# A cached-attention decode kernel on one core: V moves from SyncE's DMA queue to ScalarE's

## The chip, the core and the metric

The kernel runs on one core of a Trainium2 chip. That core has five engines with their own instruction streams: TensorE (PE, matrix products), VectorE (DVE), ScalarE (ACT), GpSimd (POOL) and SyncE (SP). Sixteen DMA engines carry data between HBM and the on-chip memory SBUF; an engine starts a transfer by an instruction in its own stream, and the transfers that one engine issues form a queue. A transfer raises a semaphore when it has landed, and any engine can wait for that. The metric is the time on the device in microseconds, as the median over runs.

## The reference: what is computed

One token for each of 4 batch entries goes through an attention block and a gated feed-forward block:

```
h  = x + softmax(q K^T / sqrt(128)) V @ wo      with q = layernorm(x) @ wq
h2 = h + (sigmoid(n @ w_gate) * (n @ w_up)) @ w_down      with n = layernorm(h)
x: [4, 1, 512]     K and V caches: [4, 32 heads, 8192, 128], bf16
```

K and V together are 537 MB of the 551 MB that the kernel reads. Every byte of them is used once.

## The kernel before, in words

The 128 pairs of batch entry and head are cut into 32 *units* of four heads (`NU`). For a unit, K is one transfer of 128 partitions by 64 KB (8.39 MB) and V is another. SBUF holds three such *slots*: K of unit u goes to slot u % 2, V to slot 2, and V of the last unit to slot 0. Slot 2 first holds the weights `wq`, slot 1 at the end `wo`, `w_gate` and `w_up`, and slot 2 at the end `w_down`.

In `unit(u)` the work of one unit is emitted in this order:

- `scores(u)`: VectorE transposes K in 16 pieces (L334), and TensorE multiplies each piece with q (L343).
- `maxima(u)`: first a tiny memset on VectorE (L360), which stands behind the last transpose and whose token `t_kd[u]` says that the K slot is free. Then the row maximum, and the exponential on ScalarE (L368).
- `pv(u - 1)`: the product of the previous unit's weights with its V, 64 matmuls on TensorE (L404), whose token is `t_pv`; ScalarE copies the result, scaled, to SBUF (L409), and TensorE collects it (L414) in two steps. The token of the first step is `t_vd[u - 1]`, that of the second is `t_ex[u - 1]`.
- `weights(u)`: VectorE transposes the exponentials into `PTz` (L374). It waits for `t_ex[u - 1]`, since the matmuls of `pv(u - 1)` read `PTz`. The transposes of the next unit's K stand behind it in VectorE's stream.

So `pv(u - 1)` needs two things: V of unit u-1 has landed, and the scores of unit u are done. The next K transposes need K landed and, by the order of VectorE's stream, `pv(u - 1)` done.

All the large transfers are issued by SyncE in one order written out by hand (L224 and L531 to L557): `wq`, K0, K1, V0, K2, V1, K3, V2 and so on to K31, V30, V31, then the later weights. SyncE works through the list in order and waits before each issue: K of unit u for `t_kd[u - 2]`, V of unit u for `t_vd[u - 1]`, V0 for `t_qp`, which says that `wq` has been used. The last V waits for `t_kd[30]`, `wo`, `w_gate` and `w_up` for `t_kd[31]`, and `w_down` for `t_vd[30]`. Because the list has one order, a K whose slot is free waits until the V ahead of it has been issued.

From unit 1 on, the streams of TensorE, VectorE and ScalarE are hardware loops: VectorE and ScalarE have 15 turns of two units each (units 1 to 30), TensorE 31 turns of one unit.

Of the kernel before, what the change touches and what calls it, by code (L numbers as in the profile page):

```python
# [18 lines left out]
class _Prog:  # L19
# [52 lines left out]
    def emit(self, eng, fn, waits=(), incs=1, ch=None):  # L72
        todo = self._waits(eng, waits)
        key = ch or eng
        tok = self.token(key, incs) if incs else None
        self._put(eng, todo, key, fn, incs, 1)
        return tok
# [41 lines left out]
def bass_sequential_preLN__mha_block_cached__glu_gated_glu__decode_kernel(  # L119
# [12 lines left out]
    B, _sq, D = A_x.shape  # L132
# [6 lines left out]
    HU = 4  # L139
    NU = B * H // HU  # L140
    R = S // 32
    SLOT = R * DH
# [11 lines left out]
    prog = _Prog({"p2d": "dve", "d2d": "dve", "a2d": "dve", "d2p": "pe", "a2p": "pe",  # L154
                  "d2a": "act", "p2a": "act",
                  "k0": "dve", "k1": "dve", "v2": "pe"})
    emit = prog.emit

    with ExitStack() as es:
# [3 lines left out]
        def raw(t):  # L163
            return t.tensor if hasattr(t, "tensor") else t
# [34 lines left out]
        def reg(slot, off, size):  # L199
            return KV[:, slot * SLOT + off:slot * SLOT + off + size]  # L200
# [20 lines left out]
        for k in keys:  # L221
            prog.sems[k] = es.enter_context(nc.semaphore("s_" + k))

        order = [("k", 0)] + [x for u in range(1, NU) for x in (("k", u), ("v", u - 1))] + [("v", NU - 1)]  # L224
        slots = {(x, u): (0 if u == NU - 1 else 2) if x == "v" else u % 2 for x, u in order}
        toks = {x: prog.token(x[0] + str(slots[x]), 16) for x in order}
        t_wq = prog.token("wq", 16)
        t_wo = prog.token("wo", 16)
        t_wg = prog.token("wg", 16)
# [64 lines left out]
        for g in range(2):  # L294
# [8 lines left out]
            t_qp = emit("pe", f, [t_wq, t_xn, t_ps0, t_selc], incs=4)  # L303

            src = bank[QB[g]].rearrange("p (k w r) -> p r k w", k=8, r=2)
# [6 lines left out]
        t_tr, t_sc, t_pv, t_ex, t_mx, t_exp, t_ptz, t_lq, t_ocp, t_rs, t_kd, t_vd, t_sum = ({} for _ in range(13))  # L312
# [4 lines left out]
        def at(ix, d):  # L317
            return ix[d] if len(ix) > d else 0
# [5 lines left out]
        def q_window(u, t=0):  # L324
            dst = bass.AP(raw(Lq), 15, [[528, 128], [128, 4], [16, 8]])
            msk = bass.AP(raw(mask), 0, [[8, 128], [0, 4], [1, 8]])
            t_lq[u] = emit("dve", lambda e, ix: e.tensor_tensor(  # L327
                dst, bass.AP(raw(q_all), at(ix, 0) * (4 * TU) + 4 * (u - TU * t), [[NU * 4, 128], [1, 4], [0, 8]]), msk, ALU.mult),
                           [t_q, t_lq0, t_mask, t_sc.get((u - 1, NT - 1))], ch="d2p")
# [51 lines left out]
        def filler(n, turns=1):  # L381
# [9 lines left out]
            if turns > 1:  # L391
                prog.close("pe")

        def pv(u, t):
            t_rs[u] = emit("dve", lambda e: e.reciprocal(rsb[:, :], bank[QB[1]][:, 1:2]), [t_sum[u]], ch="d2a")  # L395
            slot = slots["v", u]
            ob = 512 * OBK

            def f(e, ks):
                made = []  # L400
                for k in ks:
                    j, n, r4 = k % 4, k // 4, k % 4
                    lhsT = PTz[:, 512 * r4 + n:512 * r4 + n + 481:32]
                    made.append(e.matmul(PS[32 * j:32 * j + 16, ob:ob + 512], lhsT,  # L404
                                         KV[:, slot * SLOT + 512 * k:slot * SLOT + 512 * (k + 1)],
                                         start=(k < 4), stop=(k >= 60), tile_position=(0, 32 * j)))
                return made[-4:]
            t_pv[u] = emit("pe", lambda e: f(e, range(64)), [toks["v", u], t_ps0], incs=4, ch="p2a")
            t_ocp[u] = emit("act", lambda e: e.activation(O_sb, bank[OBK], ACT.Copy, scale=rsb[:, 0:1]), [t_pv[u], t_rs[u]], ch="a2p")  # L409

            def fs(e, ix, qs):
                ins = None
                for q in qs:
                    ins = e.matmul(bass.AP(raw(PS), at(ix, 0) * 4 + (512 * EX + 4 * (u - t)), [[4096, 128], [1, 4]]),  # L414
                                   O_sb[:, 128 * q:128 * (q + 1)], lane[:, q:q + 13:4],
                                   start=False, stop=(u == NU - 1 and q == 3), skip_group_check=True)
                return ins
            t_vd[u] = emit("pe", lambda e, ix: fs(e, ix, (0,)), [t_ocp[u], t_selc, t_ps0], ch="p2x")
            t_ex[u] = emit("pe", lambda e, ix: fs(e, ix, (1, 2, 3)), ch="p2d")

        def unit(u, t=0):
            scores(u)
            maxima(u)
            if u + 1 < NU:
                q_window(u + 1, t)
            else:
                emit("dve", lambda e: e.memset(dummy[:, 3:4], 0.0), ch="d2p")
            if u:
                pv(u - 1, u - 1)
            weights(u)  # L430

        emit("pe", lambda e: e.matmul(bank[EX][:, 0:128], PTz[:, 0:128], PTz[:, 0:128], start=True, stop=False,
                                      skip_group_check=True), [t_pool, t_ps0], incs=0)
        q_window(0)
        unit(0)

        prog.open("pe", "dve", "act")
        for u in range(1, NU):
            t, first = divmod(u - 1, TU)
            if u == NU - 1:  # L440
                prog.close("dve", "act")
                t = 0
            elif not first:
                prog.begin("dve", "act")
            prog.begin("pe")
            unit(u, t)
            prog.end("pe")
            if first:
                prog.end("dve", "act")
        prog.close("pe")  # L450
        filler(2, 12)
        pv(NU - 1, 0)
        t_oa = emit("dve", lambda e: e.tensor_tensor(  # L453
            OA.rearrange("p (n k) -> p n k", k=4), bass.AP(raw(PS), 512 * EX, [[4096, 128], [1, 128], [0, 4]]),
# [69 lines left out]
        for t in range(NFT):  # L524
            if t == 0:
# [4 lines left out]

        prog.dma("sp", "wq", lambda e: e.dma_start(reg(2, 0, NC * H * DH), A_wq.rearrange("(p c) f -> p (c f)", p=128)),  # L531
                 tok=t_wq)
        for n, (x, u) in enumerate(order):
            w = t_qp if n == 2 else None
            if n >= 3:
                w = t_kd[u - 2] if x == "k" else t_kd[NU - 2] if u == NU - 1 else t_vd[u - 1]
            slot = slots[x, u]
            cache = A_v_cache if x == "v" else A_k_cache
            src = cache[u // (NU // B), HU * (u % (NU // B)):HU * (u % (NU // B) + 1), :, :].rearrange("h (p r) d -> (h p) (r d)", p=32)
            prog.dma("sp", f"{x}{slot}", lambda e, src=src, slot=slot: e.dma_start(reg(slot, 0, SLOT), src), [w],  # L540
                     tok=toks[x, u])
        for _ in range(40):
            emit("sp", lambda e: e.nop(), ch="pad")
        k_done, v_done = t_kd[NU - 1], t_vd[NU - 2]
# [46 lines left out]
```

## Time and profile before

| what | value |
|---|---|
| time, median of 3 runs | 1279.48 us (1279.21 to 1279.5) |
| span of the profiled execution | 1277.7 us |
| PE busy | 797.8 us (62%) |
| DVE busy | 763.3 us (60%) |
| ACT busy | 58.9 us (5%) |
| bytes read | 550.77 MB, 431 GB/s over the span |
| share of the span in which the 16 DMA engines moved packets of SyncE's queue | 99.7% |

The span runs from the first to the last instruction that the profiler saw; the time of a run holds 1.8 us more. "Busy" counts instructions in execution. In the chain of waits each step is followed back to what released it, so a long DMA step there means that an engine waited for that transfer. A transfer's time "to landing" runs from its issue and so includes the time behind other transfers of its queue. In rows of the timeline, the brackets give the idle time ahead of an instruction and what ended it; SPq and ACTq are the streams in which SyncE and ScalarE issue transfers.

### The profile page before, as it was taken

What the parts mean: (1) busy time and instruction counts of PE and PEld (TensorE: products, weight loads), DVE (VectorE), ACT (ScalarE), POOL (GpSimd) and SP (SyncE); (2) the same over time, 40 slices, a digit from 0 to 9 for tenths busy, and PEclk for the clock granted to TensorE, in tenths of its full rate; (3) what the DMA queues carried; (4) which work ended last, traced back from release to release, by engine and by line L of the source; (5) the groups of instructions that cost most, each with busy time, mean ns of one, the idle gap of its engine ahead of it and who ended that gap; (6) DMA issues with size and microseconds to landing.
All of it is one profiled execution on the core that took longest, in us unless ns stands there. A gap on an engine that the chain in (4) does not pass through costs nothing. (4 is left out here: it accounts for less than half of the span.)

```text
span 1277.7 us, 14121 instructions
## 1 busy us (share of the span) xinstructions
PE 797.8 (62%) x4636; PEld 327.1 (26%) x4636; DVE 763.3 (60%) x917; ACT 58.9 (5%) x114; POOL 5.7 (0%) x22
## 2 busy tenths in 40 slices
PE   1676765557755557655567655567555576555578
PEld 0232222222222223222222222222222232222233
DVE  1876665556665557665567655566655566655571
ACT  2000000000000000000000000000000000000001
POOL 1000000000000000000000000000000000000000
PEclk9988877788877788877788777788777888777888
DMA  9999999999999999999999999999999999999998
GB/s 427 427 425 429 427 455 427 431 427 435 447 427 431 427 437 445 427 431 427 445 437 429 429 427 451 431 429 429 427 453 429 429 429 427 455 427 429 429 429 368
DMA packets 10244, 550.83 MB, mean 431 GB/s; under 512 B 1144, under 2 KB 1152, under 8 KB 1408
## 3 DMA queue, kind: packets, MB, share of 16 engines
q1 hardware_dynamic: 10224, 550.77, 99.7%
q8 instruction: 2, 0.03, 0.0%
q14 instruction: 2, 0.02, 0.0%
q10 hardware_dynamic: 16, 0.01, 0.0%
HBM read 550.77 MB, written 0.00 MB: 431 GB/s over the span
## 5 line engine op out<-in xcount | busy, mean ns | idle before, releaser
L334 DVE STREAM_TRANSPOSE kT<-KV 128x1024 f32<-128x1024 f32 x512 | 615.1, 1233 | 301.1 <-DMA KV<-in_A_k_cache_dram 241.0
L343 PE MATMUL PS<-kT,Lq 128*128 128x512 bf16 x2048 | 586.1, 417 | 320.2 <-DVE kT L334 302.6
L343 PEld LDWEIGHTS PS<-kT,Lq 128*128 x2048 | 209.6, 102 | 697.0 <-issue 623.6
L374 DVE STREAM_TRANSPOSE PTz<-E_sb 32x512 bf16<-32x512 bf16 x128 | 89.9, 703 | 128.9 <-PE PS L414 125.2
L404 PE MATMUL PS<-KV,PTz 128*16 128x512 bf16 x2048 | 116.9, 381 | 0.0
L378 PE MATMUL PS<-part,headw 128*128 128x2 f32 x64 | 18.7, 362 | 100.5 <-DVE PTz L374 100.5
L368 ACT ACTIVATE E_sb<-PS,negm 128x512 bf16<-128x512 f32 x32 | 22.0, 687 | 1141.2 <-DVE negm L366 1141.2
L404 PEld LDWEIGHTS PS<-KV,PTz 128*16 128x16 bf16 x2048 | 58.3, 109 | 56.8 <-issue 13.2
L414 PE MATMUL PS<-lane,kT 128*128 128x4 f32 x256 | 33.6, 255 | 30.9 <-ACT kT L409 30.9
L361 DVE TENSOR_REDUCE part<-PS 128x1 f32<-128x512 f32 x32 | 22.1, 692 | 38.8 <-PE PS L343 38.8
L414 PEld LDWEIGHTS PS<-lane,kT 128*128 128x128 f32 x256 | 31.0, 191 | 46.3 <-issue 44.9
L378 PEld LDWEIGHTS PS<-part,headw 128*128 128x128 f32 x64 | 16.0, 310 | 103.7 <-DVE PTz L374 103.7
L321 PE MATMUL PS<-Lq,headw 128*128 128x512 bf16 x32 | 18.7, 585 | 10.9 <-issue 9.5
L409 ACT ACTIVATE kT<-PS,rsb 128x512 f32<-128x512 f32 x32 | 22.0, 687 | 61.1 <-PE PS L404 61.1
L387 PE MATMUL PS<-Lq 128*128 128x512 bf16 x44 | 13.7, 478 | 0.2 <-issue 0.2
L327 DVE TENSOR_TENSOR Lq<-q_all,mask 128x32 bf16<-128x32 bf16 x32 | 9.7, 303 | 0.0
L453 DVE TENSOR_TENSOR kT<-PS,mask 128x512 bf16<-128x512 f32 x1 | 0.7, 692 | 12.9 <-PE PS L414 12.9
L366 DVE STREAM_TRANSPOSE negm<-mxr 128x32 f32<-128x32 f32 x32 | 6.8, 212 | 1.1
L363 DVE STREAM_TRANSPOSE turn<-part 128x32 f32<-128x32 f32 x32 | 6.8, 212 | 1.1
L387 PEld LDWEIGHTS PS<-Lq 128*128 128x128 bf16 x44 | 4.8, 115 | 8.2 <-issue 5.8
L395 DVE RECIPROCAL rsb<-PS 128x1 f32<-128x1 f32 x32 | 6.5, 202 | 0.7 <-PE PS L378 0.7
L300 PE MATMUL PS<-KV,kT 128*4 128x512 bf16 x32 | 3.6, 627 | 5.1 <-DMA KV<-in_A_wq_dram 5.1
(70 smaller groups left out, 59.5 us busy)
## 6 DMA issues: line engine op xcount, KB each, us to landing
KV<-in_A_wq_dram SPq DMA_DIRECT2D x1, 4096.0 KB, 12.2
KV<-in_A_wo_dram SPq DMA_DIRECT2D x1, 4096.0 KB, 27.5
KV<-in_B_w_gate_dram SPq DMA_DIRECT2D x1, 1792.0 KB, 31.4
KV<-in_B_w_up_dram SPq DMA_DIRECT2D x1, 1792.0 KB, 35.2
KV<-in_B_w_down_dram SPq DMA_DIRECT2D x1, 1024.0 KB, 32.5
KV<-in_A_k_cache_dram SPq DMA_DIRECT2D x32, 49.8
KV<-in_A_v_cache_dram SPq DMA_DIRECT2D x32, 30.8
KV<-in_B_w_down_dram SPq DMA_DIRECT2D x1, 512.0 KB, 33.3
```

What stands on the lines that cost most here:

```text
L321: emit("pe", lambda e: e.matmul(bank[bk], headb, zeros, start=True, stop=False, skip_group_check=True), waits, incs=0)
L327: t_lq[u] = emit("dve", lambda e, ix: e.tensor_tensor(dst, bass.AP(raw(q_all), at(ix, 0) * (4 * TU) + 4 * (u - TU * t), [[NU * 4, 128], [1 ...
L334: t_tr[u, c] = emit("dve", lambda e: e.transpose(kT[:, (c % 2) * TW:(c % 2 + 1) * TW], KVw[:, o:o + TW]), w, ch="d2p")
L343: ins = e.matmul(bank[SBK], bass.AP(raw(Lq), ix[-1] * 2 + (128 * t + c % 2), [[528, 128], [1, 128]]), rhs, start=False, stop=False, skip_g ...
L361: a = emit("dve", lambda e: e.tensor_reduce(part[:, 0:1], bank[SBK], AX.X, ALU.max), [t_sc[u, NT - 1], t_pool], ch="d2d")
L368: t_exp[u] = emit("act", lambda e: e.activation(E_sb[:, :], bank[SBK], ACT.Exp, bias=negm[:, 0:1], scale=SCALE, accum_out=part[:, 1:2]), [ ...
L374: return [e.transpose(PTz[32 * q:32 * (q + 1), :].rearrange("p (r q c) -> p r q c", r=4, q=4)[:, :, q, :], E_sb[32 * q:32 * (q + 1), :].re ...
L378: t_sum[u] = emit("pe", lambda e: e.matmul(bank[QB[1]][:, 0:2], headw[:, :], part[:, 0:2], start=True, stop=True), [t_ptz[u], t_selc], ch= ...
L387: emit("pe", lambda e: [e.matmul(bank[XS], Lq[:, 0:128], Lq[:, 0:512], start=True, stop=True) for _ in range(n)][-1], [t_ps0, t_lq[NU - 1] ...
L404: made.append(e.matmul(PS[32 * j:32 * j + 16, ob:ob + 512], lhsT, KV[:, slot * SLOT + 512 * k:slot * SLOT + 512 * (k + 1)], start=(k < 4), ...
L409: t_ocp[u] = emit("act", lambda e: e.activation(O_sb, bank[OBK], ACT.Copy, scale=rsb[:, 0:1]), [t_pv[u], t_rs[u]], ch="a2p")
L414: ins = e.matmul(bass.AP(raw(PS), at(ix, 0) * 4 + (512 * EX + 4 * (u - t)), [[4096, 128], [1, 4]]), O_sb[:, 128 * q:128 * (q + 1)], lane[: ...
```

## The change

A helper `load` issues one K or V transfer, or a range of columns of it, from a chosen engine. ScalarE issues V0 (with the wait for `t_qp`) ahead of unit 0, and V of unit u+1 inside `pv(u)`, between the 64 matmuls and ScalarE's own copy of their result, with the wait for `t_pv[u]` in place of `t_vd[u]`; this goes up to V28. SyncE issues `wq`, all of K without a V in between, then V29, the first half of V31, V30 and the second half of V31, and then the later weights as before. ScalarE's stream is no longer in the loop of 15 turns: it is unrolled. The slots are as before.

```diff
-        order = [("k", 0)] + [x for u in range(1, NU) for x in (("k", u), ("v", u - 1))] + [("v", NU - 1)]
+        order = [(x, u) for u in range(NU) for x in "kv"]
         slots = {(x, u): (0 if u == NU - 1 else 2) if x == "v" else u % 2 for x, u in order}
-        toks = {x: prog.token(x[0] + str(slots[x]), 16) for x in order}
+        toks = {x: prog.token(x[0] + str(slots[x]), 16 + 16 * (x == ("v", NU - 1))) for x in order}
+        APART = NU - 3
...
+        def load(eng, x, u, w, a=0, b=SLOT):
+            slot = slots[x, u]
+            cache = A_v_cache if x == "v" else A_k_cache
+            src = cache[u // (NU // B), HU * (u % (NU // B)):HU * (u % (NU // B) + 1), :, :].rearrange("h (p r) d -> (h p) (r d)", p=32)
+            prog.dma(eng, f"{x}{slot}", lambda e: e.dma_start(reg(slot, a, b - a), src[:, a:b]), [w], tok=toks[x, u])
...
             t_pv[u] = emit("pe", lambda e: f(e, range(64)), [toks["v", u], t_ps0], incs=4, ch="p2a")
+            if u + 1 < APART:
+                load("act", "v", u + 1, t_pv[u])
             t_ocp[u] = emit("act", lambda e: e.activation(O_sb, bank[OBK], ACT.Copy, scale=rsb[:, 0:1]), [t_pv[u], t_rs[u]], ch="a2p")
...
+        load("act", "v", 0, t_qp)
         q_window(0)
         unit(0)
 
-        prog.open("pe", "dve", "act")
+        prog.open("pe", "dve")
...
-        for n, (x, u) in enumerate(order):
-            w = t_qp if n == 2 else None
-            if n >= 3:
-                w = t_kd[u - 2] if x == "k" else t_kd[NU - 2] if u == NU - 1 else t_vd[u - 1]
...
+        for u in range(NU):
+            load("sp", "k", u, t_kd[u - 2] if u > 1 else None)
+        load("sp", "v", NU - 3, t_vd[NU - 4])
+        load("sp", "v", NU - 1, t_kd[NU - 2], 0, SLOT // 2)
+        load("sp", "v", NU - 2, t_vd[NU - 3])
+        load("sp", "v", NU - 1, t_kd[NU - 2], SLOT // 2)
```

More of the change, by code (lines that the diff above doesn't have):

```diff
@@ L440, in bass_sequential_preLN__mha_block_cached__glu_gated_glu__decode_kernel @@
             if u == NU - 1:
-                prog.close("dve", "act")
+                prog.close("dve")
                 t = 0
             elif not first:
-                prog.begin("dve", "act")
+                prog.begin("dve")
             prog.begin("pe")
@@ L448, in bass_sequential_preLN__mha_block_cached__glu_gated_glu__decode_kernel @@
             if first:
-                prog.end("dve", "act")
+                prog.end("dve")
         prog.close("pe")
@@ L532, in bass_sequential_preLN__mha_block_cached__glu_gated_glu__decode_kernel @@
                  tok=t_wq)
-        for n, (x, u) in enumerate(order):
-            w = t_qp if n == 2 else None
-            if n >= 3:
-                w = t_kd[u - 2] if x == "k" else t_kd[NU - 2] if u == NU - 1 else t_vd[u - 1]
[L537 to L541, printed above, removed]
+        for u in range(NU):
[4 more added lines that the diff above has]
+        load("sp", "v", NU - 1, t_kd[NU - 2], SLOT // 2)
         for _ in range(40):
```

## The prediction

> **What bounds the kernel now.** I read the page first, then busy time by stages, SyncE's waits, and the chain of waits.
>
> ```profile
> span 1277.7 us, 14121 instructions
> ...
> DMA  9999999999999999999999999999999999999998
> ...
> q1 hardware_dynamic: 10224, 550.77, 99.7%
> ```
>
> The 16 DMA engines move packets of one queue for 99.7% of the span. In three stretches of whole units (the last two columns are DMA share and GB/s):
>
> ```profile
> 100.00:138.70 38.70, 23.88 (x137) 9.92 (x138) 23.02 (x29) 1.47 (x3) 0.00 (x0) 0.78 1.00 434
> 500.00:887.00 387.00, 240.95 (x1392) 99.56 (x1392) 235.25 (x282) 14.65 (x30) 0.00 (x0) 0.81 1.00 434
> 1000.00:1193.50 193.50, 120.79 (x694) 49.76 (x694) 117.74 (x141) 7.32 (x15) 0.00 (x0) 0.81 1.00 434
> ```
>
> Always 1.00 and 434 GB/s, while PE, DVE and ACT have room. SyncE's longest wait looks like a fault that the change would mend, K held back behind V:
>
> ```profile
> SPq L540 <- PE PS L414: 1124.4, 30, 38.5
> ```
>
> The chain of waits shows that it costs nothing:
>
> ```profile
> 1008.94 0.33 SPq L540
> 1009.27 0.04 issue
> 1009.31 49.78 DMA KV<-in_A_k_cache_dram
> ...
> 1241.51 33.33 DMA KV<-in_B_w_down_dram
> 1274.84 0.04 issue
> ```
>
> One unit of the timeline (transposes of K26, `pv(25)`, the issues of V26 and K28, the landing of K27), then the landing of K31:
>
> ```profile
> 1020.41 2.37 DVE L334 STREAM_TRANSPOSE kT<-KV 128x1024 f32<-128x1024 f32 x2 [7.82 <-DMA KV<-in_A_k_cache_dram]
> 1041.04 0.06 DVE L360 MEMSET dumm<- 128x1 f32 x1
> 1042.20 3.65 PE L404 MATMUL PS<-KV,PTz 128*16 128x512 bf16 x64
> 1045.98 0.69 ACT L409 ACTIVATE kT<-PS,rsb 128x512 f32<-128x512 f32 x1 [1.45 <-PE PS L404]
> 1047.24 0.33 SPq L540 DMA_DIRECT2D KV<-in_A_v_cache_dram  x1
> 1047.61 0.43 SPq L540 DMA_DIRECT2D KV<-in_A_k_cache_dram  x1
> 1047.98 2.90 DVE L374 STREAM_TRANSPOSE PTz<-E_sb 32x512 bf16<-32x512 bf16 x4 [4.04 <-PE PS L414]
> 1059.12 2.37 DVE L334 STREAM_TRANSPOSE kT<-KV 128x1024 f32<-128x1024 f32 x2 [8.23 <-DMA KV<-in_A_k_cache_dram]
> ...
> 1213.92 2.37 DVE L334 STREAM_TRANSPOSE kT<-KV 128x1024 f32<-128x1024 f32 x2 [7.60 <-DMA KV<-in_A_k_cache_dram]
> ```
>
> From the landing of K26 (1020.41) to that of K31 (1213.92) are five units: 38.70 us each, so F = 19.35 us for one load of 8.39 MB, 433.5 GB/s. K27, issued at 1009.31 behind V25, takes 49.78 us to land: 11.1 for the rest of K26, then 2 F = 38.7. Nothing is left over, so the queue never runs dry; when a K is issued, 11 us of work still lie ahead of it. All 550.77 MB at that rate take 1270.5 us, and from the first issue of `wq` (0.80, quoted below) to the last landing (1274.84) are 1274.0. Only 3.5 us could be saved by keeping the engines fed, and they lie at the start. The order of issues has nothing more to give; it can only open gaps, or change the rate.
>
> **The change part by part.** I ask of each edit whether the engines run dry. I assume that two queues with work share an engine evenly (all K and V packets are alike) and that the sum stays 433.5 GB/s. From K's issue without V in its way, SyncE issues K28 at `t_kd` (1041.1) instead of 1047.61: 6.5 us earlier into a queue that had 11 us of work. Worth 0.
>
> *The start.* Rows that carry it:
>
> ```profile
> 0.80 0.56 ACTq L234 DMA_DIRECT2D KV<-in_A_x_dram  x1
> 0.80 0.38 SPq L531 DMA_DIRECT2D KV<-in_A_wq_dram  x1
> 2.86 0.68 DVE L272 BATCH_NORM_STATS2 kT<-KV 4x6 f32<-4x512 bf16 x1 [2.86 <-DMA KV<-in_A_x_dram]
> 13.01 3.58 PE L300 MATMUL PS<-KV,kT 128*4 128x512 bf16 x32 [5.06 <-DMA KV<-in_A_wq_dram]
> 16.71 0.33 SPq L540 DMA_DIRECT2D KV<-in_A_v_cache_dram  x1
> 32.32 2.37 DVE L334 STREAM_TRANSPOSE kT<-KV 128x1024 f32<-128x1024 f32 x2 [14.25 <-DMA KV<-in_A_k_cache_dram]
> 53.34 0.06 DVE L360 MEMSET dumm<- 128x1 f32 x1
> 53.43 0.33 SPq L540 DMA_DIRECT2D KV<-in_A_k_cache_dram  x1
> 59.80 2.37 DVE L334 STREAM_TRANSPOSE kT<-KV 128x1024 f32<-128x1024 f32 x2
> 80.82 0.06 DVE L360 MEMSET dumm<- 128x1 f32 x1
> 91.53 1.25 DVE L334 STREAM_TRANSPOSE kT<-KV 128x1024 f32<-128x1024 f32 x1 [0.86 <-DMA KV<-in_A_k_cache_dram]
> ```
>
> The price a of a queue that starts empty: `x` (4 KB) takes 2.06 us from issue to use; `wq` (4.19 MB, 9.68 us at the rate) takes 12.21, so 2.5. I take 2.1 to 2.5.
>
> Before, V0 is issued at 16.71 but lies behind K0 and K1. Now it has its own queue and shares with K0 from 16.7 + 2.1 = 18.8. K0 started F before its landing, at 12.95; 5.85 of its 19.35 us are done, the other 13.5 take 27.0. K0 lands at 45.8 instead of 32.3. Unit 0's weights end 27.5 us after K0 lands (59.80 - 32.32): 73.3. K1 lands when the bytes of K0, V0 and K1 are through, at 12.95 + 3 F = 71.0, before that. The transposes of K1 run from 73.3 and free their slot 21.0 later (80.82 - 59.80): 94.3, where it was 80.8. K3 needs that slot; its first data come at 94.4 + a = 96.5 to 96.9. What lies ahead is the same work as before (`wq`, K0, K1, V0, K2), so K2 lands at 91.5 as before. V1 can't fill the gap: it waits for `pv(0)`, which needs the scores of unit 1 and ends at 94.3 + 1.2 + 3.65 = 99.1. **The engines stand idle from 91.5 to 96.5 or 96.9: 5.0 to 5.4 us, taken as 5.2.** The work that covered V1's late issue, V0 still in the queue, is gone.
>
> *The steady units.* Let p be the end of `pv(u-1)`. ScalarE issues V(u) there, 1.4 us earlier than SyncE did (1047.24, where L404 ends at 1045.85). Behind the issue on ScalarE stands the copy L409, and behind that L414, L374 and the next transposes, so all come 0.56 us later (the issue of `x` on ScalarE); no DMA engine waits for that if a queue has work. `PTz` is done at p + 5.0 + 0.56 (1050.88 - 1045.85), the next slot is free 20.7 us later (1041.04 - 1020.41): p + 26.3. A gap opens if V(u) and the rest r of K(u+2) are through before that, so when r < 26.3 - F = 6.95. After the start K has been alone from `t_kd` until V's first data: 1.16 (1042.20 - 1041.04) + 3.65, so r = 14.5. K and V then share; V still has F - r left when K(u+3) joins, shares again, and K runs alone for 3.65 + a, so the next r is 14.5 - 5.95 = 8.6. From there the same working gives r' = 26.3 - 3.65 - 2.3 - r = 11.8, then 8.6, 11.8 and so on. Always above 6.95: **no gap, 0 us**, units alternating long and short with the mean at 38.7. The margin is 1.6 us, thin.
>
> *ScalarE unrolled.* Apart from the new issues it executes the same instructions with the same waits; 0 us here. K2 lands 59.2 us after K0 where 3 F are 58.05, so something once cost 1.15 us; I keep that as the upper bound for fetching a longer stream.
>
> *The end.* V29 goes behind K31 with the old wait. When it lands at L, V30 may be issued at L + 5.05 (1047.24 - 1042.20), and the first half of V31 fills the queue to L + 9.7. That covers it by 4.6 us. The second half of V31 then runs to L + 38.7; `wo`, which waits for `t_kd[31]`, is issued near L + 29.5. No gap. After the last V come the same weights, and the end follows the last landing as now. 0 us.
>
> **Sum** against the profiled execution: 1277.7 + 5.2 = 1282.9; the median of the runs is 1.8 above its span, so 1284.7.
>
> *A rule on the rate.* The Trainium skill (DMA: Bandwidth & Descriptors, "Where 436 GB/s comes from") gives 435.2 GB/s as the ceiling of the 16 ports; the trace's 433.5 lies 0.4% under it. By that page an estimate for a perfect second queue is 1265.5 us in place of 1270.5, so 5.0 back and a sum of 1279.7.
>
> **The rivals.**
>
> *Whole loads take turns.* An engine might finish one queue's load before it turns to the other. Then V0 goes between K0 and K1: K0 lands at 32.3, K1 at 71.0, its slot is free at 92.0, K3's data come at 94.2 to 94.6, and the gap is 2.9: 1282.4. For it: nothing in the views, which show no engine with two full queues. The Trainium skill has the rule (DMA: Bandwidth & Descriptors, "Queues, rings and completion order"): an engine drains a packet of several descriptors from one ring before it switches. No run here shows how large such a packet is. 12%.
>
> *The early V0 costs nothing*: K0 and K1, long in the queue, go first. K1's slot is free at 80.8, K3 in time, and the result is 1279.5. 7%.
>
> *The rate rises a little.* From K31's landing to that of `w_down`, V30, V31 and the weights (26.48 MB) take 60.92 us, 434.7 GB/s. Over the 1180 us in which two queues run (18.8 to about 1200), 0.28% is 3.3 us: 1281.4. 14%.
>
> *The rate rises enough: faster.* Two queues could leave no pause between two packets of an engine. It decides from 5.2 + 2.6 = 7.8 us on, so 0.66% or 436.4 GB/s; at 437.5 the time is 1273.9. Against: three stretches of one to ten units all show 434, as a hard limit would. For: the DMA share of 1.00 says that packets lie end to end, not that each could not be quicker. 10%.
>
> *V gets less than half, or two queues disturb each other.* At 45 to 55, V has only 11.9 us done when K(u+2) ends; the rest shares with K(u+3), K alone takes 5.95 again, the next r is 4.3, and 2.65 us of gap open in every second unit; at the start K0 lands earlier and the gap there is 2.9: 15 x 2.65 + 2.9 = 43, 1322. V with more than half only lengthens the start. And if sharing cost 2% (1.15 in 58.05, the one lag seen), 24 us come on top: 1308. Half such a disturbance gives 1296. For: the margin of 1.6 us. Against: the packets of K and V are alike. 17%.
>
> **How the numbers follow.** The forecast (even sharing, the same rate) has 40%, with 1282.5 to 1287 as its own range. Two tenths of a per cent, 2.6 us, is about what these runs can tell from no change: faster is below 1276.9, slower above 1282.0. Faster: the 10% of the higher rate and 2 for no gap with a slightly higher rate. Same: 14 - 1 for the small rise, 7 - 1 for the free start, 5 of the whole loads. Slower: the rest, 64. The range leaves out most of the faster case below and the heavier half of the disturbances above: 1276.5 to 1296.
>
> **What would show it.** Right: K0 lands near 46, the first transposes of K1 start near 73, and the DMA row or a window over 90 to 98 us shows a hole of some 5 us; from 100 us on the stretches of two units show 434 GB/s and 1.00, alternating short and long; the last landing stands 2.9 us ahead of the end. Wrong: 434 replaced by another figure in those stretches (a rate that depends on the number of queues), holes that recur every second unit (uneven shares), or K0 landing still at 32 (no early sharing).

## The result and the profile after

The changed kernel takes 1321.74 us in the median (1320.39 to 1324.57), the kernel before 1279.35: a ratio of 1.0336, with a 95% interval of 1.0324 to 1.0348. It is 42.4 us slower. The forecast was 1284.7, the range ended at 1296: the direction was right and the size far too small.

The page of the changed kernel, in the same parts as shown of before:

```profile
span 1320.6 us, 13984 instructions
...
DMA  9989999999999999999999999999999999998995
...
q1 hardware_dynamic: 6192, 307.50, 54.6%
q10 hardware_dynamic: 4192, 243.28, 42.6%
```

Two queues now carry the bytes: q1 is SyncE's, with K, the last V loads and the weights, and q10 is ScalarE's, with V0 to V28. Together they are busy for 97.2% of the span in place of 99.7%. VectorE's wait for the collected product with V (the transposes of the weights behind L423) has grown to three times. In the waits of the changed kernel, with total, times and longest:

```profile
DVE PTz L375 <- PE PS L423: 387.9, 31, 22.3
```

and of the kernel before:

```profile
DVE PTz L374 <- PE PS L414: 125.2, 31, 4.2
```

Busy time by stages of the changed kernel (the last two columns are DMA share and GB/s) shows four places where time went:

```profile
88.00:98.00 10.00, 8.52 (x84) 3.52 (x82) 5.91 (x12) 0.98 (x3) 0.00 (x0) 1.00 0.57 216
98.00:1200.00 1102.00, 675.57 (x3778) 278.10 (x3807) 652.02 (x772) 40.06 (x82) 0.00 (x0) 0.81 0.99 423
1200.00:1212.00 12.00, 10.17 (x94) 4.54 (x92) 7.03 (x13) 1.47 (x3) 0.00 (x0) 1.00 0.68 273
1308.00:1320.60 12.60, 9.05 (x108) 3.52 (x100) 3.88 (x10) 3.77 (x7) 0.00 (x0) 0.99 0.01 5
```

The same long stretch of the kernel before, and its last 12.6 us:

```profile
98.00:1200.00 1102.00, 691.34 (x3988) 284.60 (x3990) 675.59 (x804) 41.79 (x86) 0.00 (x0) 0.81 1.00 433
...
1265.10:1277.70 12.60, 8.27 (x88) 2.89 (x80) 3.87 (x10) 3.77 (x7) 0.00 (x0) 1.00 0.68 283
```

- *The start*, 88 to 98 us: a share of 0.57 is a hole of 4.3 us.
- *The steady units*, 98 to 1200: 423 GB/s against 433. The bytes moved at 423 would have taken 1102 x (1 - 423/433) = 25.4 us less at 433.
- *Between K30, V28 and K31*, 1200 to 1212: a share of 0.68, 3.8 us lost.
- *The end*: all but 0.06 MB has been moved by 1308, and 12.6 us of work follow, at 5 GB/s. Before, the last 12.6 us still moved 283 GB/s, so 12.6 x (283 - 5)/433 = 8.1 us are new.

These are estimates from rounded shares and rates; their sum is 41.6, and the spans differ by 42.9. The trace also lists every packet (for K and V a packet is the 64 KB row of one partition, and takes 2.42 us in the kernel before). Counted from these records, with the bytes of a packet spread over its time and held against 433.5 GB/s, 4.6 us are lost up to 98 us, 26.5 from there to 1200, 3.6 from there to 1308, and 8.2 more than before behind that: 42.9.

The long stretch is not slow evenly. Two stretches of 20 us with a hole in each, and the 140 us between them, which run at the old rate:

```profile
640.00:660.00 20.00, 14.04 (x109) 6.43 (x107) 13.88 (x21) 1.47 (x3) 0.00 (x0) 0.91 0.89 367
660.00:800.00 140.00, 84.89 (x450) 34.33 (x455) 81.71 (x94) 4.39 (x9) 0.00 (x0) 0.81 1.01 434
800.00:820.00 20.00, 13.56 (x107) 6.40 (x107) 13.88 (x21) 1.47 (x3) 0.00 (x0) 0.92 0.87 367
```

The holes come every 159 us, that is every four units, which take 154.8 us at 38.7 each. By its rate (367 against 433) such a hole costs 3 us, though no engine moves anything for only 1.8 to 1.9 us (648.4 to 650.3 and 807.1 to 808.9 in the packet records): the engines stop and start one after the other, and the first packet of each after the hole takes 2.4 to 3.5 us, most of them over 3, in place of 2.42. Halfway between two holes, where SyncE's queue has run empty and ScalarE's is about to, about 1 us more is lost. One turn of such a cycle in the timeline, from the issue of V17 to the product with V18 (between 733 and 815 us):

```profile
733.10 0.34 ACTq L399 DMA_DIRECT2D KV<-in_A_v_cache_dram  x1
...
775.89 5.25 PE L411 MATMUL PS<-KV,PTz 128*16 128x512 bf16 x64 [14.86 <-DMA KV<-in_A_v_cache_dram]
781.28 0.34 ACTq L399 DMA_DIRECT2D KV<-in_A_v_cache_dram  x1
...
786.60 2.37 DVE L335 STREAM_TRANSPOSE kT<-KV 128x1024 f32<-128x1024 f32 x2
807.83 0.06 DVE L361 MEMSET dumm<- 128x1 f32 x1
808.99 3.65 PE L411 MATMUL PS<-KV,PTz 128*16 128x512 bf16 x64
```

V17 takes 42.8 us from issue to use, because it shares the DMA engines with K. TensorE waits 14.86 us for it. From its landing, the product, the collection, the weights and the transposes of K19 take until 807.83; only then is the next K slot free. By that time K20 and V18 are both through, so nothing is queued.

The packet records give the time from the issue to the first data, which no view shows:

```
issue of          at us      first data after
K17               649.37     0.96 us    (both queues empty)
V17               733.10     3.36 us    (K19 running)
V18               781.28     3.54 us    (K20 running)
V1 to V28         28 issues  3.4 to 5.7 us, median 3.9 (K running)
```

### The profile page after: what moved, and what is told of

It reads as the page before. It is cut to its first block, busy times and chain, and to the rows that moved or that the text cites. A ratio compares the mean times of both kernels' runs of the same rounds, so it can differ in the third digit from the quotient of the medians.

```text
span 1320.6 us, 13984 instructions
## 1 busy us (share of the span) xinstructions
PE 804.1 (61%) x4588; PEld 330.9 (25%) x4636; DVE 761.6 (58%) x917; ACT 59.0 (4%) x114; POOL 5.7 (0%) x22
## 2 busy tenths in 40 slices
DMA packets 10389, 550.83 MB, mean 417 GB/s; under 512 B 1160, under 2 KB 1168, under 8 KB 1424
## 5 line engine op out<-in xcount | busy, mean ns | idle before, releaser
L344 PE MATMUL PS<-kT,Lq 128*128 128x512 bf16 x2048 | 580.1, 413 | 134.8 <-DVE kT L335 116.6
L411 PE MATMUL PS<-KV,PTz 128*16 128x512 bf16 x2048 | 147.9, 453 | 218.8 <-DMA KV<-in_A_v_cache_dram 218.8
L411 PEld LDWEIGHTS PS<-KV,PTz 128*16 128x16 bf16 x2048 | 62.6, 118 | 303.8 <-DMA KV<-in_A_v_cache_dram 230.1
L423 PE MATMUL PS<-lane,kT 128*128 128x4 f32 x256 | 33.9, 256 | 41.7 <-ACT kT L418 41.7
L423 PEld LDWEIGHTS PS<-lane,kT 128*128 128x128 f32 x256 | 31.2, 192 | 57.0 <-issue 55.6
L362 DVE TENSOR_REDUCE part<-PS 128x1 f32<-128x512 f32 x32 | 22.1, 691 | 38.7 <-PE PS L344 38.7
L388 PE MATMUL PS<-Lq 128*128 128x512 bf16 x27 | 11.0, 463 | 2.8 <-issue 2.3
L322 PEld LDWEIGHTS PS<-Lq,headw 128*128 128x128 bf16 x32 | 3.5, 108 | 13.1 <-issue 11.6
L365 DVE TENSOR_SCALAR_CACHE_REDUCE turn<-turn 128x32 f32<-128x32 f32 x32 | 6.0, 186 | 1.1
## 6 DMA issues: line engine op xcount, KB each, us to landing
KV<-in_A_v_cache_dram SPq DMA_DIRECT2D x2, 4096.0 KB, 26.3
```

The source lines that it names most:

```text
L344: ins = e.matmul(bank[SBK], bass.AP(raw(Lq), ix[-1] * 2 + (128 * t + c % 2), [[528, 128], [1, 128]]), rhs, start=False, stop=False, skip_g ...
L362: a = emit("dve", lambda e: e.tensor_reduce(part[:, 0:1], bank[SBK], AX.X, ALU.max), [t_sc[u, NT - 1], t_pool], ch="d2d")
L388: emit("pe", lambda e: [e.matmul(bank[XS], Lq[:, 0:128], Lq[:, 0:512], start=True, stop=True) for _ in range(n)][-1], [t_ps0, t_lq[NU - 1] ...
```

## The experiments

All are variants of the changed kernel unless said otherwise; the kernel before, run beside them, took 1279.0 to 1279.2 us.

**A warm TensorE ahead of the late product.** In the row at 775.89 the 64 matmuls take 5.25 us in place of 3.65, after 14.86 us of idling. That lengthens the chain, so the first theory was that it opens the holes.

```diff
             ob = 512 * OBK
...
+            if u % 2 and u < NU - 1:
+                prog.open("pe")
+                for _ in range(10):
+                    prog.begin("pe")
+                    emit("pe", lambda e: [e.matmul(bank[XS], headb, PTz[:, 0:512], start=True, stop=True) for _ in range(4)][-1], incs=0)
+                    prog.end("pe")
+                prog.close("pe")
             t_pv[u] = emit("pe", lambda e: f(e, range(64)), [toks["v", u], t_ps0], incs=4, ch="p2a")
```

> The changed kernel, with 40 idle-running matmuls on TensorE ahead of the product with V in every second unit (those whose V is late; its profile shows TensorE idle 9 to 15 us there and the 64 matmuls behind such a wait at 5.3 to 5.8 us instead of 3.65). Theory A (the chain from V's landing to the next free K slot is too long, because TensorE comes out of the wait slow, so both queues run empty about 4 us in every four units): the chain shortens by 2 to 3 us, the holes of the steady units go, and some 25 of the 42 us come back: 1293 to 1298. Theory B (two queues cost transport time whatever the engines do: a queue that joins waits 3.4 to 5.7 us for its first data, each landing takes a turn): 1319 to 1323.

Measured: 1319.18 us (1.0313, 1.0296 to 1.0331). But the fillers ended 4 to 7 us early and the product behind them was still slow, 4.9 to 6.3 us, so this didn't try the theory. (Here TensorE's loop has two units per turn, so that the fillers stand in every second one only.) With 60 fillers (`range(15)`):

> As the first kernel with filler matmuls, but 60 in place of 40, so that they end 1 to 2 us ahead of the late V instead of 6 (there the product with V still took 4.9 to 5.8 us). If the slow product behind the wait is a part of what empties the queues (chain from V's landing to the next slot 1.6 to 2.2 us shorter): the holes shrink from 4 us per four units to 1 or 2, 1298 to 1310. If it has no part: 1317 to 1321.

Measured: 1317.4 us (1.0301, 1.0279 to 1.0323). The product took 3.65 us in 27 of 32 units now; the groups of that kernel show 403 ns a matmul (453 in the changed kernel, 381 before):

```profile
L411 PE MATMUL PS<-KV,PTz 128*16 128x512 bf16 x2048 | 126.3, 403 | 34.9 <-DMA KV<-in_A_v_cache_dram 34.7
```

So a fast product in nearly every unit brings back some 4 of the 42 us, with one reserve: where V came early, the fillers themselves held the product up. That the slow product alone opens the holes fell with this.

**K in halves, reloaded half by half.**

```diff
+                if c == NT // 2 - 1:
+                    t_kh[u] = emit("dve", lambda e: e.memset(dummy[:, 1:2], 0.0), ch="d2x")
...
-            load("sp", "k", u, t_kd[u - 2] if u > 1 else None)
+            load("sp", "k", u, t_kh[u - 2] if u > 1 else None, SLOT // 2, SLOT)
+            load("sp", "k", u, t_kd[u - 2] if u > 1 else None, 0, SLOT // 2, "y")
```

> The changed kernel, with each K loaded as two halves, each with its own semaphore; a half is reloaded as soon as its own eight transposes are done, so SyncE's queue is refilled 10 us earlier in every unit. Theory A (K's queue runs empty before its slot is free): no holes from 90 us on, at the start neither; what stays is the end, 7 to 10 us: 1286 to 1290. Theory B (every joining queue costs): twice as many landings and joins of K, so no gain, 1319 to 1335.

Measured: 1290.68 us (1.0090, 1.0073 to 1.0107), 0.7 over the 1290 of theory A: 31 of the 42 us are back. The long stretch of this kernel stands at the old rate, still with two queues:

```profile
98.00:1200.00 1102.00, 735.88 (x3911) 288.58 (x3911) 668.68 (x821) 41.05 (x84) 0.00 (x0) 0.83 1.00 433
```

That excludes that two queues at work lower the rate by themselves. But the edit does two things: it refills K's queue earlier, and it makes K's packets 32 KB long beside V's 64 KB. The control keeps the short packets and the old time of issue:

```diff
-            load("sp", "k", u, t_kh[u - 2] if u > 1 else None, SLOT // 2, SLOT)
+            load("sp", "k", u, t_kd[u - 2] if u > 1 else None, SLOT // 2, SLOT)
```

> Control for K in halves: K is again two transfers with 32 KB packets, but both halves wait for the last transpose, so nothing is issued earlier than in the changed kernel; only K's packets are half as long. Theory R (K in halves helped because SyncE's queue was refilled 10 us earlier): the gain goes, 1313 to 1323. Theory S (an engine takes packets of the two queues in turn whatever their size, so half-size K packets give V two thirds while both run, and a joining V waits half as long): the gain stays, 1288 to 1293.

Measured: 1293.56 us (1.0114, 1.0097 to 1.0130), 0.6 over theory S's interval and 19 under theory R's. Its long stretch:

```profile
98.00:1200.00 1102.00, 728.30 (x3888) 289.68 (x3918) 671.09 (x823) 41.01 (x84) 0.00 (x0) 0.83 1.00 433
```

The short packets are worth 28 us, and the earlier refill 2.9 beside them; with long packets it was not tried. So the refill that theory A of the run before named is the smaller part of its gain. The opposite edit gives V the short packets:

```diff
-                load("act", "v", u + 1, t_pv[u])
+                load("act", "v", u + 1, t_pv[u], 0, SLOT // 2)
+                load("act", "v", u + 1, t_pv[u], SLOT // 2)
```

> The changed kernel with every V (V0 to V30) as two transfers with 32 KB packets and K whole. Theory S (packets in turn): V gets one third of the engine while K runs, K is through early, then V runs alone, lands, and both queues stand empty until the next slot is free, in every unit or two: a reckoning packet by packet from the measured durations gives 140 to 190 us more than the kernel before, 1420 to 1470. Theory R (only the time of K's refill counts) or a fair split by bytes: 1315 to 1330.

Measured: 1425.21 us (1.1142, 1.1120 to 1.1165; two runs), within the 1420 to 1470 that packets in turn should give. The long stretch has lost a tenth of its rate:

```profile
98.00:1200.00 1102.00, 609.35 (x3442) 251.00 (x3467) 587.61 (x699) 36.62 (x75) 0.00 (x0) 0.79 0.91 386
```

The bytes and the queues are the same in three kernels, and the length of one queue's packets differs: with packets of K and V in the ratio 1:2, 1:1 and 2:1 the times are 1293.56, 1321.74 and 1425.21 us. The packet records show the split itself: where both queues keep starting packets (counted in steps of 2.5 us), V has 66%, 50% and 32% of the bytes.

**Both in halves.** Here the packets are equal again, and half as long.

> The changed kernel with K and V both as two transfers with 32 KB packets, nothing issued earlier: packets of both queues are equal again, so the split is even as in the changed kernel, but a packet lasts 1.2 us in place of 2.4. Theory S1 (it is the split that matters): the loss of the steady units stays, 1313 to 1323. Theory S2 (with an even split it is the waits of one to two packets, which a joining queue and each landing pay, that use up the margin): these waits halve; the reckoning packet by packet gives 8 to 16 us over the kernel before, 1288 to 1298, 9 of them at the end.

Measured: 1320.75 us (1.0325, 1.0309 to 1.0341), as in the changed kernel, with V at 51% where both queues run. The even split keeps the loss with either length of packets, though it lies elsewhere: the start loses nothing more than before, and the long stretch loses more.

```profile
98.00:1200.00 1102.00, 700.19 (x3815) 281.69 (x3812) 655.09 (x800) 39.62 (x81) 0.00 (x0) 0.81 0.98 420
```

K has a semaphore for each half here, as in the two versions with K in halves, so the gain there didn't come from transposes that start on the first half. The run doesn't free the joining wait from blame, as I had meant it to: its packet records show 3.4 to 4.1 us from V's issue to its first data, so the wait had not halved with the packets.

**A shorter chain.** The split stays even; the last quarter of each K is left out of the scores.

```diff
-    NT = R * DH // 2 // TW
+    NT = R * DH // 2 // TW - 4
```

> The changed kernel with whole K and V, the even split and all transfers kept, but the last quarter of each K is left out of the scores (12 transposes and products per unit in place of 16): every K slot is free about 5 us earlier after V's landing. Theory A (the holes come because the chain from V's landing to the next free K slot, 34 to 36 us in the profile, is longer than the transfers still queued): the holes of the steady units go and the end's chain is shorter too, 1282 to 1291. Theory B (two whole-packet queues lose transport time by themselves): 1305 or more.

Measured: 1293.88 us (1.0113, 1.0097 to 1.0130), 3 us over the upper end of theory A's interval and 11 under theory B's. The long stretch is at 430 GB/s:

```profile
98.00:1200.00 1102.00, 613.01 (x3453) 244.60 (x3454) 526.91 (x675) 41.05 (x84) 0.00 (x0) 0.76 1.00 430
```

So the holes are a race between the chain that frees the next K slot and the transfers still queued; with the chain 5 us shorter no full hole is left (430 GB/s), and with the larger share for V neither (433).

**V0 from SyncE, behind K1.**

```diff
-        load("act", "v", 0, t_qp)
...
             load("sp", "k", u, t_kd[u - 2] if u > 1 else None)
+            if u == 1:
+                load("sp", "v", 0, t_qp)
```

> The changed kernel, with V0 issued from SyncE behind K0 and K1 as before. Theory A and B: the hole near 91 us (2.9 us, and about 1 us of slow first packets) goes; the steady units and the end stay: 1312 to 1318. If the start were worth the 5.2 us of the prediction and nothing else moved: 1316.5.

Measured: 1311.86 us (1.0255, 1.0238 to 1.0272), 9.9 less than the changed kernel and just under the forecast. That is more than the hole at the start, and the long stretch is no better:

```profile
98.00:1200.00 1102.00, 692.41 (x3812) 278.10 (x3810) 654.48 (x778) 40.33 (x83) 0.00 (x0) 0.81 0.99 423
```

The profiled spans differ by 9.1 us; counted from the packet records, 4.6 of them lie at the start, 0.8 in the long stretch and 3.7 behind 1200 us. The holes come at other times here, and why the end gained was not tried.

**The end alone**, with everything up to K30 and V28 in SyncE's queue in the old order:

```diff
-            if u + 1 < APART:
-                load("act", "v", u + 1, t_pv[u])
...
             load("sp", "k", u, t_kd[u - 2] if u > 1 else None)
+            if 0 < u < NU - 2:
+                load("sp", "v", u - 1, t_vd[u - 2] if u > 1 else t_qp)
```

> All loads on SyncE's queue in the old order up to K30 and V28 with the old waits, ScalarE's stream unrolled as in the change, and only the new end: K31, V29, half of V31, V30, the other half. Theory A (a part of the loss lies at the end: V29 behind K31 makes the last K transposes wait for the product with V29, and from the last free K slot the remaining chain takes 42 us as before): 8 to 11 us over the kernel before, 1288 to 1291. Theory B (all of the loss comes from two queues at work): 1279 to 1281.

Measured: 1288.35 us (1.0071, 1.0055 to 1.0088). One queue, no holes, and 9.2 us lost at the end. Its long stretch:

```profile
98.00:1200.00 1102.00, 690.15 (x3945) 283.93 (x3944) 676.20 (x805) 41.81 (x86) 0.00 (x0) 0.81 1.00 433
```

Since this kernel also has ScalarE's stream unrolled, that part was tried alone in the kernel before:

> The kernel before with ScalarE's stream unrolled and nothing else. Every theory: no change, 1278.5 to 1280.0. If the longer stream costs something, it is a part of the 9 us that were put down to the new end.

Measured: 1279.0 us against 1279.07 (1.0001, 0.9991 to 1.0010). Nothing.

**No fillers at the end.** The 24 matmuls ahead of the last product (`filler(2, 12)`) are left out of the changed kernel.

> The changed kernel without the 24 filler matmuls ahead of the last product with V. If the end is bound by the chain from the last free K slot and no longer by transfers (V31 is there some 10 us before its product starts at 1297.2; the weights of unit 31 are done at 1288.5): 5 to 7 us less, reduced by a slower TensorE behind the pause, 1314 to 1318. If the last landing still bounds the end: 1321 to 1323.

Measured: 1313.49 us (1.0272, 1.0254 to 1.0289), 8.2 less and 0.5 under the forecast. The timeline of this run, with the last free K slot and the last product:

```profile
1276.94 0.06 DVE L361 MEMSET dumm<- 128x1 f32 x1
...
1287.54 5.42 PE L411 MATMUL PS<-KV,PTz 128*16 128x512 bf16 x64
```

The product starts 10.6 us after the slot is free, where it took 18.6 with the fillers (1297.17 - 1278.60), although it is slow here. In the changed kernel the end is bound by this chain and not by a landing.

**Halves with the old end.** K in halves as above, and V29 ahead of K31, V30 ahead of V31, all four from SyncE.

> The changed kernel with K in halves, each half reloaded as soon as it is free, and with the old order at the end (V29 ahead of K31, then V30, then V31 in its halves). If the start, the split of packets and the end are all there is, the two queues now lose nothing: 1279 to 1282, the same as the kernel before. If two queues cost transport time beside these, it stays 5 us or more above, 1285 or more.

Measured: 1290.96 us (1.0095, 1.0080 to 1.0110): a miss. There are no holes up to 1160 us, but a new one follows:

```profile
98.00:1160.00 1062.00, 708.73 (x3770) 277.92 (x3771) 644.81 (x792) 39.62 (x81) 0.00 (x0) 0.83 1.00 433
1174.00:1186.00 12.00, 6.37 (x79) 3.28 (x77) 4.21 (x13) 1.47 (x3) 0.00 (x0) 1.00 0.29 98
```

By the share of 0.29 some 8.5 us are lost there. Read from the order of the streams: V29 waits in SyncE's stream for the product with V28, K31 stands behind V29, and ScalarE's queue has nothing more. That this order is the cause was not tried by another edit. None of the versions with two queues, nor the new end alone, comes down to the kernel before.

## Why the prediction was wrong, step by step

**The bound and what could be won: right.** The kernel before had 3.5 us to give, and no version with two queues found any of it. The rate with two queues is the old one where neither queue runs dry (433 GB/s in the kernel with K in halves), so both rivals with a higher rate are out. The Trainium skill (DMA: Bandwidth & Descriptors, "Issuing engines are not separate DMA queues") says that transfers of all issuing engines run on the same 16 DMA engines and that a second issuer saves only the time to issue; these runs agree, 433 against 433.

**The start: right in mechanism, the hole a little too large.** The timeline of the changed kernel shows K0 ready, K1's first transposes and K1's slot free:

```profile
44.54 2.37 DVE L335 STREAM_TRANSPOSE kT<-KV 128x1024 f32<-128x1024 f32 x2 [26.34 <-DMA KV<-in_A_k_cache_dram]
...
71.70 2.37 DVE L335 STREAM_TRANSPOSE kT<-KV 128x1024 f32<-128x1024 f32 x2
...
92.47 0.06 DVE L361 MEMSET dumm<- 128x1 f32 x1
```

Forecast were 45.8, 73.3 and 94.3 with a hole of 5.0 to 5.4; measured is a hole of 4.3 to 4.6. In the packet records the engines are empty from 90.66 to 93.53, 2.9 us, since K3's first data come 0.96 us after its issue and not 2.1 to 2.5; the rest lies in engines that stop earlier or start later, and in slow first packets. The even split from the moment V0 joins is what the forecast assumed, and the rivals "whole loads take turns" (K0 at 32.3) and "the early V0 costs nothing" are out. The Trainium skill (DMA: Bandwidth & Descriptors, "Queues, rings and completion order") says that an engine drains a packet of several descriptors from one ring before it switches. Here a load's share of an engine is 8 packets of 64 KB as the trace lists them; K0's landing at 44.5, and that both queues start packets in every 2.5 us while both run, fit a turn of a packet or so, not one of the whole share.

**The steady units: wrong.** The step that failed is "always above 6.95: no gap, 0 us". 25.4 us were lost there. The term that was mis-sized is the 5.95 us that lie between the last data of one V and the first data of the next, in which K runs alone: 3.65 for the product and 2.3 for a queue that starts. In the changed kernel's packet records it is 7.6 to 14.2 us (V1 to V28). From V17 to V18, the turn shown above, it is 11.7:

- V17's last data is through at 773.12, and its semaphore is complete at 775.85, 2.7 us later; the forecast had nothing for this.
- The product and the issue take 5.4 us, to 781.28. Behind a wait of 15 us the product took 5.25 where the forecast had 3.65.
- V18's first data come 3.5 us after the issue, where the price a was 2.1 to 2.5. That price was set for every issue; measured are 0.96 us with both queues empty and 3.4 to 5.7 with the other one running.

So K20 is that much further on, and at V18's first data (784.82) only r = 2.9 us of it are left, where the forecast had 8.6 or more. The two loads are through at 784.82 + 19.35 + 2.9 = 807.1; the slot is free at 807.83, 26.55 us after the issue (26.3 in the forecast), and K21's first data come at 808.88: a hole of 1.8 us. The margin was 1.6 us, and I called it thin but gave it no chance of its own. Which part used it up is not settled: in this turn the late semaphore alone is 2.7 us, the product 1.6 and the joining wait some 1.2; making the product fast brought back 4 us in all, and the other two couldn't be changed by themselves. Shown is that the race is lost with the even split, nearly won with a chain 5 us shorter and won with packets of V twice as long as K's.

**The end: wrong, and it could have been read.** "After the last V come the same weights, and the end follows the last landing as now. 0 us." In the kernel before, the last K slot is free here (its timeline):

```profile
1234.94 0.06 DVE L360 MEMSET dumm<- 128x1 f32 x1
```

From there to the end of the span are 42.8 us of work, just as long as the transfers then needed: the old end was balanced, and I took only one side of it into the sum. The same side after:

```profile
1246.84 5.29 PE L411 MATMUL PS<-KV,PTz 128*16 128x512 bf16 x64 [9.53 <-DMA KV<-in_A_v_cache_dram]
...
1257.21 2.37 DVE L335 STREAM_TRANSPOSE kT<-KV 128x1024 f32<-128x1024 f32 x2
...
1278.60 0.06 DVE L361 MEMSET dumm<- 128x1 f32 x1
...
1297.17 3.65 PE L411 MATMUL PS<-KV,PTz 128*16 128x512 bf16 x64
```

The last transposes wait for the product with V29, which now lands behind K31, and the slot is free 31.8 us after V29's landing (29.5 in the forecast). 42.0 us follow, as before. With the forecast's own L: L + 29.5 + 42.8 = L + 72.3 against L + 38.7 + 22.2 + 2.9 = L + 63.8 for the transfers (22.2 is the rest of the 60.92 quoted in the prediction), 8.5 us that the sum should have held. The end alone measured 9.2.

**The rival that named the number.** "V gets less than half" was priced at 1322 us, and 1321.74 was measured. It was not that rival: its holes were 2.65 us in every second unit from an uneven split, and measured are about 4 us per four units, 3 of them in one hole, with an even split, plus 8 to 9 us at the end that it didn't have. That the two numbers agree is luck. Its direction was right, though: with V's packets half as long as K's the time is 1425.

**ScalarE unrolled: right**, worth nothing (1.0001). That K's earlier issue was worth nothing was not tried by itself; beside short packets the still earlier refill by halves was worth 2.9 us.

## What to carry to other kernels

Where transfers bound a kernel and a queue is never empty, its order is a schedule; here, splitting it into two queues gave the order away to turns by packet, and the share of each stream then followed the length of its packets. Before such a change, write down for each buffer the chain from a landing to the next issue and compare it with the work that is still queued then: a margin of 1.6 us in 39 was none here. At the end of a kernel compare both sides, the transfers left and the chain of work left, since a balanced end hides either of them.

## What the runs showed of the hardware

- A V load that joined while K was running had its first data 3.4 to 5.7 us after the issue (changed kernel, V1 to V28, median 3.9); K17, issued with both queues empty, 0.96 us. With packets of half the length on both queues V still waited 3.4 to 4.1.
- From the last data of a V load to its complete semaphore passed 2.7 to 2.9 us where K was running, and 0.3 to 0.5 where K was not, or had just begun (changed kernel).
- After a hole the first packet of each engine took 2.4 to 3.5 us, most of them over 3, in place of 2.42 (changed kernel, 808.88 and 650.33 us).
- Two queues share by packets in turn: V has 66%, 50% and 32% of the bytes with K's packets half as long as V's, equal, and twice as long, and the kernels take 1293.56, 1321.74 and 1425.21 us.
- In the changed kernel the 64 matmuls of a product took 3.65 us where TensorE had idled less than 1 us before, and 5.01 to 6.26 after 9.5 to 15.4 us.
